# A folded weight made by seven half-block products a row pair, on one Trainium2 core

## The chip, the cores and the metric

The kernel runs on one core of a Trainium2 chip (trn2). A time is the device time of one execution in microseconds, and a comparison is made between medians of runs. A profile shows one execution, taken by the hardware profiler. Its engines are TensorE (PE; PEld is its weight load), VectorE (DVE), ScalarE (ACT), GpSimd (POOL) and SyncE (SP, which issues most of the DMAs).

## The reference, cut to what matters

An mLSTM cell (batch 4, 8 heads, 768 positions, 40 wide) is followed by a feed-forward block with a multiplicative gate. Only the second part is touched by the change:

```python
def _moe_ref(x, w1, w2, w3, w_out):      # x is 3072 x 320, the cell's output
    a = x @ w1                           # 320 x 1024
    b = x @ w2                           # 320 x 1024
    h = a * b @ w3                       # 1024 x 1024
    return (h @ w_out).astype(np.float32)  # 1024 x 320
```

As nothing stands between `@ w3` and `@ w_out`, the kernel multiplies the two weights first. `w3 @ w_out`, 1024 x 320, is the folded weight; each token block is then multiplied by it once. All products are in float32.

## The kernel before, in words

**Steps.** The program is written out by one Python loop over `s`, 32 steps. The cell's work is cut in 24 units (6 stretches of 128 positions for each of 4 batches); step `s` makes the attention-like products of unit `s` and the outputs of unit `s − 1`. These small products of 64x64 quarters of TensorE's array, `quarter_work`, write the tiles `cell`. They stand at the end of a step on TensorE and need, from GpSimd, the weighted values `vw` (line 330), the masked weights `pw` (L308) and decayed states (L335, `decayed`). On VectorE they lead to `h`, `den`, the output `y`, and the states (L404, L414). `x_trans` turns a finished `y` on TensorE into `px`, and ScalarE copies that to `xT`, the feed-forward input.

**Up blocks.** In steps 2 to 15 each step also makes one or two up blocks (`up`, `up_rest`). A block is two of the eight 128-wide parts of the hidden dimension for 256 tokens. `pa` and `pb` collect `x @ w1` and `x @ w2`. The model width is 320 = 128 + 128 + 64: the first two parts are products of 128 rows (`up`), the last 64 rows are four products on 64x64 quarters of the array that run together (`up_rest`, tile `wr`). ScalarE then copies `pa` to `a_sb` (L638), and VectorE multiplies `pb` by it into `ab` (L639). In steps 19 to 30 the up blocks are made in another way, by seven half-block products (`up_by_seven`), and the last output blocks too (`out_by_seven`). Neither is touched.

**Fold.** Weights come by DMA as raw words; ScalarE scales them and VectorE puts them together to float32 (`convert`, L199 and L200), a few in each step by the list `n_cvt`. For `w3` VectorE also turns the block (L248) into `w3T`, of which two are kept, one for each of two 128-row parts `ko`. Some steps later, at the start of a step, `fold` makes 8 products of 128 x 128 by 128 x 320 for each `ko` whose `w3T` is ready, in one PSUM bank `wp`, and ScalarE copies the sum to `w3o` (L264). There are 8 such `ko`; two are folded at the start of step 10 and one in each of the steps 11 to 16. `wo` holds `w_out`, and after the fold its memory serves as workspace.

**Down blocks.** From step 16 on, `ffn_out` multiplies `ab` by `w3o`: 8 products of 320 columns a block of 128 tokens, in a bank `po`, copied by ScalarE to `o_sb` and sent out by its queue.

**Order.** TensorE's instructions are issued in the order of the program text (`in_order`, through the helpers `mm`, L92, and `transpose`, L95). On the other engines a scheduler keeps nearly the order of the text as well; `tc.issue_after` holds a group of instructions behind a named one. Four PSUM banks belong to `cell`, and four are handed out by `mps`, each new tile taking a bank that has been emptied; a tile's first product waits for the engine that emptied that bank. A float32 product of the text is two matmuls and two weight loads in TensorE's stream.

The lines that hand out the work around the change:

```python
n_up = [0] * 2 + [1] * 4 + [2] * 10 + [0] * 16
n_down = [0] * 16 + [2] * 5 + [1] * 4 + [0] * 7
todo = w12[5:] + [("wo", i, 0) for i in range(FO)] + [("w3", ko, part) for ko in range(FO) for part in range(2)]
n_cvt = [0, 0, 2, 0, 1, 2, 3, 3, 3] + [2] * 6
```

Of the kernel before, what the change touches and what calls it, by code (L numbers as in the profile page):

```python
# [8 lines left out]
FP = mybir.dt.float32  # L9
# [3 lines left out]
UP = 2.0 ** 9  # L13
# [3 lines left out]
def kernel(  # L17
# [212 lines left out]
    w3T_t = {}  # L230
    turned_w3, ready_w3 = [], []

# [4 lines left out]
    def convert():  # L237
        if not scaled:
            scale_next()
        dst, raw, ko, half = scaled.pop(0)  # L240
        if dst is not None:
            to_f32(dst, raw)
            return
        w3 = wst.tile([128, CW], FP, name="w3", tag="w3")
        to_f32(w3, raw)
        if half == 0:
            w3T_t[ko] = wst.tile([128, FO, 128], FP, name="w3T", tag="w3T")
        nc.vector.transpose(out=w3T_t[ko].rearrange("c k (m r) -> c m k r", r=32)[:, 2 * half:2 * half + 2],  # L248
                            in_=w3.rearrange("r (m c k) -> r m k c", m=2, k=FO))
        if half:  # L250
            turned_w3.append(ko)

    def fold():
        while ready_w3:
            w3_mm(ready_w3.pop(0))
        ready_w3.extend(turned_w3)
        turned_w3.clear()

    def w3_mm(ko):
        w3T = w3T_t.pop(ko)  # L260
        wp = mps([128, DM], "wp")
        for ki in range(FO):
            mm(wp, w3T[:, ki, :], wo[:, ki, :], start=(ki == 0), stop=(ki == FO - 1))
        nc.scalar.mul(out=w3o[:, ko, :], in_=wp, mul=UP ** -2)  # L264

# [351 lines left out]

    def up(gr, fs, cs):

# [3 lines left out]
        x, n = x_t[gr], cs.stop - cs.start  # L623
        pa, pb = mps([128, len(fs), n], "pa"), mps([128, len(fs), n], "pb")
        for p, wt in ((pa, w1), (pb, w2)):
# [4 lines left out]

    def up_rest(pa, pb, x, gr, fs, cs):
        for i, f in enumerate(fs):
            for j, e in quarters:
                mm((pa, pb)[j][halves[e], i, :], wr[halves[j], f * 128 + e * L:f * 128 + (e + 1) * L],
                   x[halves[j], KF, cs], start=False, stop=(i == len(fs) - 1))
        j, t0 = divmod(cs.start, 2 * P)
# [95 lines left out]

    def ffn_out(blocks, pos=None):

        pos = pos or [mps([P, DM], "po") for _ in blocks]
        for (gr, j), po in zip(blocks, pos):
            for f in range(FO):
                mm(po, ab_t[gr][j // 2][:, f, j % 2 * P:(j % 2 + 1) * P], w3o[:, f, :], start=(f == 0), stop=(f == FO - 1))
        for (gr, j), po in zip(blocks, pos):
            o_sb = ffn.tile([P, DM], FP, name="o_sb", tag="o_sb", bufs=2)  # L740
            nc.scalar.copy(out=o_sb, in_=po)  # L741
            t0 = j * S + gr * P
            nc.scalar.dma_start(out=out[t0:t0 + P, :], in_=o_sb)


    KH, NH = FO // 2, DM // 2

# [9 lines left out]
    T_o, S_o = [], {}  # L757
    wsums = out_weight_sums()

# [53 lines left out]
    todo = w12[5:] + [("wo", i, 0) for i in range(FO)] + [("w3", ko, part) for ko in range(FO) for part in range(2)]  # L813
    n_cvt = [0, 0, 2, 0, 1, 2, 3, 3, 3] + [2] * 6
    n_fetch = [5, 5, 10]
# [4 lines left out]
    for s in range(len(n_up)):  # L820
# [21 lines left out]
        if s < NU:  # L842
            if s >= B:
                decayed(state[s % B][1], state[s % B][0], s, 0)
        if s == 2 or N_DVE < s < NY + 2:
            twice(s - 2)
        if NY <= s - 2 < NU:
            get_back(s - 2)
        while s >= N_DVE and turned < min(s - 2, NY):
            x_trans(turned)  # L850
            turned += 1
        fold()
        if s >= len(n_up) - 2:
# [16 lines left out]
        if seven and s <= NU:  # L870
            ffn_out([downs.pop(0) for _ in range(n_down[s])], [cell[1][:, i, 0:DM] for i in range(2)])
        else:
            for _ in range(n_down[s]):
                ffn_out([downs.pop(0)])
# [4 lines left out]
        now = [ups.pop(0) for _ in range(n_up[s])]  # L879
        open_ups = [up(*x) for x in now] if s != 2 else []  # L880
        if s == 3:
            turn(3)
        def rest():
            for x in open_ups:
                up_rest(*x)
            if seven:
# [5 lines left out]
        def between():  # L892
# [17 lines left out]
            convert()  # L910
            up_rest(*block)

# [3 lines left out]
        else:  # L916
            rest()
        with tc.issue_after(gated.ins) if gated else nullcontext():
            if seven:
                seven[3]()  # L920
            for _ in range({NU: 1, NU + 1: 3}.get(s, 0)):
                next(wsums)
# [41 lines left out]
        if s == B:  # L964
            for i, r in enumerate(third):
                nc.sync.dma_start(out=U_d[i * GC:(i + 1) * GC].rearrange("c r t -> r c t"), in_=U3[r])
        with tc.issue_after(gated.ins) if N_DVE <= s + 1 < NU else nullcontext():
            for _ in range(n_cvt[s] if s < len(n_cvt) else 0):
# [13 lines left out]
    behind.close()  # L982
    assert not ups and not sevens and not downs and not outs and not summed and not todo and not pend and not turned_w3 and not ready_w3, (len(ups), len(downs), len(todo), len(pend))
# [28 lines left out]
```

## Time and profile before

| | us |
|---|---|
| median of 3 runs (lowest, highest) | 426.75 (425.93, 427.64) |
| the profiled execution, its own time | 427.89 |
| span of that execution, first to last instruction | 425.8 |

Busy time of the engines in four stretches of that span:

| stretch, us | PE | DVE | ACT | POOL | DMA share |
|---|---|---|---|---|---|
| 0 to 108 (steps 0 to 9) | 100.98 | 83.34 | 70.04 | 34.64 | 0.91 |
| 108 to 218 (steps 10 to 16) | 109.12 | 80.72 | 41.45 | 24.14 | 0.73 |
| 218 to 334 (steps 17 to 26) | 115.58 | 82.34 | 29.48 | 59.07 | 0.51 |
| 334 to 426 (the rest) | 88.37 | 67.07 | 9.12 | 36.45 | 0.08 |

A busy time is the time in which at least one instruction of the engine was under way. Matmuls overlap, so the mean duration of one says less than the spacing of their starts. "Idle before, releaser" in a row is the time for which the engine stood still ahead of that group, and what ended it; "issue" is a stand for which the profile shows no reason. The fold runs from 108 to 209 us.

### The profile page before, as it was taken

The numbers are of one execution on the slowest core, as the hardware profiler recorded it, in microseconds if no ns is written. First come the engines' busy times: TensorE is split into PE (matmuls) and PEld (weight loads), VectorE is DVE, ScalarE is ACT, GpSimd is POOL, SyncE is SP. The second block draws the span as 40 slices with busy tenths as digits, with TensorE's granted clock in tenths as the row PEclk, the third lists the DMA queues.
The fourth block names the chain that finished last, engine by engine and source line by source line (L and its number), as shares of the span: only waits on it lengthen the run. The fifth ranks groups of instructions, "written<-read, shape, count | busy, mean of one in ns | idle before, by whom it ended". The sixth has DMA issues, their size and how long they took to land.

```text
span 425.8 us, 13079 instructions
## 1 busy us (share of the span) xinstructions
PE 414.1 (97%) x5353; PEld 335.3 (79%) x5353; DVE 313.5 (74%) x635; ACT 150.1 (35%) x404; POOL 154.3 (36%) x211
## 2 busy tenths in 40 slices
PE   7989989999999999999999999999999999999996
PEld 4768878888688788787777778788778879888896
DVE  6676986888949779778736966596868699575971
ACT  4766865567723623630433313032311110210000
POOL 4421342233303303303307751546453587542100
PEclk9989999999999999999999999999999999999999
DMA  8999998598977776985425675756421120000001
GB/s 186 204 173 245 214 144 140 134 193 180 215 183 154 166 182 135 181 164 105 89 80 130 153 141 121 142 133 117 87 44 36 35 39 2 31 2 31 2 32 62
DMA packets 135211, 51.15 MB, mean 120 GB/s; under 512 B 109360, under 2 KB 126960, under 8 KB 135152
## 3 DMA queue, kind: packets, MB, share of 16 engines
q1 hardware_dynamic: 131552, 46.29, 53.9%
q10 hardware_dynamic: 3600, 4.03, 2.7%
q8 instruction: 42, 0.69, 0.7%
q14 instruction: 17, 0.14, 0.1%
HBM read 44.50 MB, written 5.80 MB: 118 GB/s over the span
## 4 chain that ended last, share of the span: by engine, by line
PE 53%; issue 20%; DVE 7%; POOL 7%; SPq 7%; DMA 5%; ACT 1%; POOLq 0%; DVEq 0%
PE cell L92 17%; PE pa L92 12%; PE o L92 8%; PE pb L92 8%; PE p L92 3%; POOL pw L308 3%; SPq L184 3%; DVE w3T L666 2%; PE pt L95 1%; POOL vw L330 1%; SPq L148 1%; DMA raw<-in_moe_w_dram 1%; PE fill L92 1%; POOL raw L659 1%; POOL state L335 1%
## 5 line engine op out<-in xcount | busy, mean ns | idle before, releaser
L335 POOL TENSOR_TENSOR state<-state,decay 128x164 f32<-128x164 f32 x40 | 20.0, 500 | 154.8 <-DVE state L404 129.0
L92 PE MATMUL pa<-xT,w 128*128 128x256 f32 x240 | 60.4, 382 | 0.0
L92 PEld LDWEIGHTS pa<-xT,w 128*128 128x128 f32 x240 | 44.4, 190 | 6.8 <-DVE h L430 0.4
L303 ACT ACTIVATE pw<-pw,aT 128x64 f32<-128x64 f32 x184 | 46.4, 339 | 3.2 <-ACT o_sb L741 1.9
L92 PE MATMUL pb<-xT,w 128*128 128x256 f32 x192 | 45.4, 379 | 0.0
L729 POOL TENSOR_TENSOR ab<-ab,a_sb 128x512 f32<-128x512 f32 x22 | 29.4, 1356 | 32.2 <-DVE ab L684 32.2
L92 PEld LDWEIGHTS pb<-xT,w 128*128 128x128 f32 x192 | 36.4, 190 | 5.0
L711 POOL TENSOR_TENSOR wo<-wo 128x512 f32<-128x512 f32 x22 | 27.4, 1268 | 29.8 <-DVE wo L686 29.8
L92 PE MATMUL pa<-xT,wr 64*64 64x256 f32 x384 | 37.0, 386 | 0.5 <-DVE wr L200 0.5
L92 PE MATMUL wp<-wo,w3T 128*128 128x320 f32 x128 | 35.9, 433 | 1.1 <-DVE ab L639 0.6
L308 POOL TENSOR_SCALAR_AFFINE_SELECT pw<-pw 64x512 f32<-64x512 f32 x48 | 35.8, 746 | 3.0 <-ACT pw L303 1.2
L92 PE MATMUL pb<-xT,wr 64*64 64x256 f32 x384 | 36.4, 380 | 0.0
L92 PE MATMUL cell<-w3o,ab 128*128 128x320 f32 x128 | 35.4, 432 | 0.0
L638 ACT ACTIVATE a_sb<-pa 128x512 f32<-128x512 f32 x24 | 14.3, 598 | 59.0 <-PE pb L92 59.0
L639 DVE TENSOR_TENSOR ab<-pb,a_sb 128x512 f32<-128x512 f32 x24 | 16.4, 688 | 23.2 <-ACT a_sb L638 22.8
L92 PEld LDWEIGHTS wp<-wo,w3T 128*128 128x128 f32 x128 | 23.8, 190 | 10.5 <-DVE ab L639 0.8
L92 PEld LDWEIGHTS cell<-w3o,ab 128*128 128x128 f32 x128 | 24.3, 190 | 9.5
L92 PEld LDWEIGHTS pa<-xT,wr 64*64 64x64 f32 x384 | 18.9, 132 | 15.4 <-issue 8.8
L686 DVE SCALAR_TENSOR_TENSOR a_sb<-pa,wo 128x512 f32<-128x512 f32 x12 | 8.3, 689 | 29.8 <-PE pa L92 29.8
L430 DVE TENSOR_TENSOR h<-cell,h 64x164 f32<-64x164 f32 x88 | 28.6, 326 | 1.6
L92 PE MATMUL po<-w3o,ab 128*128 128x320 f32 x96 | 26.4, 433 | 0.0
L92 PEld LDWEIGHTS po<-w3o,ab 128*128 128x128 f32 x96 | 18.1, 190 | 7.3
(180 smaller groups left out, 846.4 us busy)
## 6 DMA issues: line engine op xcount, KB each, us to landing
raw<-in_moe_w_dram SPq DMA_DIRECT2D x64, 128.0 KB, 3.4
kbuf<-in_k_dram SPq DMA_DIRECT2D x24, 160.0 KB, 4.5
v_all<-in_v_dram SPq DMA_DIRECT2D x24, 160.0 KB, 4.9
o_in<-in_o_gate_dram SPq DMA_DIRECT2D x24, 160.0 KB, 4.8
pw<-U_d SPq DMA_DIRECT2D x28, 128.0 KB, 3.5
raw<-in_moe_w_dram SPq DMA_DIRECT2D x5, 512.0 KB, 6.7
raw<-in_moe_w_out_dram SPq DMA_DIRECT2D x8, 320.0 KB, 4.1
gates<-in_k_dram SPq DMA_DIRECT2D x28, 80.0 KB, 2.5
```

Of the source, the lines that this page charges most:

```text
L92: in_order(nc.tensor.matmul(out, lhsT=lhsT, rhs=rhs, start=start, stop=stop))
L184: nc.sync.dma_start(out=dst, in_=src)
L303: nc.scalar.activation(out=pw[:, h, :], in_=src[:, h, :], func=AF.Exp, bias=aT[:, c, b * H + h:b * H + h + 1])
L308: nc.gpsimd.affine_select(out=pw[r], in_=pw[r], compare_op=OP.is_ge, fill=0.0, base=0, pattern=[[0, H], [1, L]], channel_multiplier=-1)
L335: nc.gpsimd.tensor_tensor(out=new, in0=old, op=OP.mult, in1=decay[:, b * NP:(b + 1) * NP, 2 * c + x:2 * c + x + 1] .to_broadcast([P, NP, D1]))
L430: nc.vector.tensor_tensor(out=part, in0=ph[x][halves[e]], in1=part, op=OP.add)
L638: nc.scalar.mul(out=a_sb, in_=pa, mul=UP ** -2)
L639: nc.vector.tensor_tensor(out=ab_t[gr][j][:, fs[0]:fs[-1] + 1, t0:t0 + a_sb.shape[-1]], in0=pb, in1=a_sb, op=OP.mult)
L666: nc.vector.tensor_tensor(out=dst, in0=p, in1=q, op=OP.subtract)
L686: nc.vector.scalar_tensor_tensor(out=out, in0=p, scalar=UP ** -2, in1=q, op0=OP.mult, op1=OP.add)
L711: aside_by.tensor_tensor(out=kept[j][:, 1:4:2], in0=kept[j][:, 1:3], in1=kept[j][:, 3:4].to_broadcast([128, 2, TH]), op=OP.add)
L729: aside_by.tensor_tensor(out=t[:, f:FO:FH, :], in0=t[:, f:FO:FH, :], in1=a, op=OP.mult)
```

## The change

The product of two consecutive 128-row parts of `w3` (a row pair) and `w_out` is cut in 2 x 2 by 2 x 2 half blocks (`A11` to `A22`, `B11` to `B22`). Before, it took eight half-block products for a pair, as sixteen products of 320 columns; now it takes seven, each of four products of 160 columns.

- Sums of weights on both sides are needed. Those of `w_out` (`T1` to `T4`, four of 640 columns) are made by GpSimd after steps 8 and 9; the last of them is made again in another place in step 15. Those of a row pair (`S1` to `S4`, four of 512 columns) are made by GpSimd after steps 9, 11, 13 and 15. `S3` and `T3` overwrite parts of `w3T` and `wo`; the rest lie in `fold_m`, `w3o`, and memory of `ab` and `raw` that is free then.
- `fold_first` makes two products after the quarter work of steps 9, 11, 13, 14; ScalarE copies them to `w3o`.
- `fold_second` makes the other five in steps 10, 12, 14, after the first up block has been finished, and in step 16 between the down blocks. ScalarE copies the products to memory, and five additions, by GpSimd (VectorE in step 16), make the rows of `w3o`. In step 16 the last two of eight parts of the two down blocks wait for them and stand after the quarter work.
- In steps 9, 11 and 13 the banks of the up blocks are handed out as `pa`, `pa`, `pb`, `pb` instead of `pa`, `pb`, `pa`, `pb`.
- In steps 2 to 5 the quarter products of up blocks are split in two of 128 columns each: both parts in steps 2 to 4, the second part alone in step 5.
- One weight conversion moves from step 8 to step 5, the buffer `w3` becomes single, and `o_sb` moves to the memory of `fold_m`.

```diff
-    def fold():
-        while ready_w3:
-            w3_mm(ready_w3.pop(0))
...
-        for ki in range(FO):
-            mm(wp, w3T[:, ki, :], wo[:, ki, :], start=(ki == 0), stop=(ki == FO - 1))
-        nc.scalar.mul(out=w3o[:, ko, :], in_=wp, mul=UP ** -2)
+    def fold_weight_sums():
...
+        for dst, p, q in ((T1, B12, B11), (T2, B22, T1), (T4, B21, T2), (B12, B22, B12)):
+            yield nc.gpsimd.tensor_tensor(out=dst, in0=p, in1=q, op=OP.subtract)
+    def fold_sums(i):
...
+        for dst, p, q, op in ((S1, A21, A22, OP.add), (S2, S1, A11, OP.subtract), (A21, A11, A21, OP.subtract),
+                              (S4, A12, S2, OP.subtract)):
+            nc.gpsimd.tensor_tensor(out=dst, in0=p, in1=q, op=op)
+    def fold_first(i):
...
+        wp = fold_products(((A11, B11), (A12, B21)))
+        return lambda: nc.scalar.mul(out=fold_of(i)[:, 0:3:2], in_=wp, mul=UP ** -2)
+    def fold_last_sum():
...
+        nc.gpsimd.tensor_tensor(out=B21, in0=B21, in1=fold_T[1], op=OP.subtract)
+    def fold_second(i):
...
+        wp, wq = mps([128, 3, NH], "wp"), mps([128, 2, NH], "wq")
+        for p, x, a, b, first, last in ((wq, 1, A22, T4, True, False), (wp, 0, S1, T1, True, False), (wp, 1, S2, T2, False, False),
+                                        (wp, 2, S3, T3, False, True), (wq, 0, S4, B22, False, True)):
+            for k in range(KH):
+                mm(p[:, x], a[:, k, :], b[:, k, :], start=(first and k == 0), stop=(last and k == KH - 1))
...
+        nc.scalar.mul(out=M1, in_=wp, mul=UP ** -2)
+        nc.scalar.mul(out=M2, in_=wq, mul=UP ** -2)
+        def adds(by=nc.gpsimd):
+            for out, p, q in ((C[:, 1], M1[:, 1], C[:, 0]), (C[:, 0], C[:, 0], C[:, 2]), (C[:, 2], M1[:, 2], C[:, 1]),
+                              (C[:, 1:4:2], C[:, 1:3], M1[:, 0:1].to_broadcast([128, 2, NH])), (C[:, 1:3], M2, C[:, 1:3])):
+                by.tensor_tensor(out=out, in0=p, in1=q, op=OP.add)
...
+    def up_banks(n):
+        shape = [128, 2, 2 * P]
+        return zip(*[[mps(shape, name) for _ in range(n)] for name in ("pa", "pb")])
...
+            parts = split[i]
+            n = (cs.stop - cs.start) // parts
+            for t in range(parts):
+                for j, e in quarters:
+                    mm((pa, pb)[j][halves[e], i, t * n:(t + 1) * n], wr[halves[j], f * 128 + e * L:f * 128 + (e + 1) * L],
...
-    n_cvt = [0, 0, 2, 0, 1, 2, 3, 3, 3] + [2] * 6
+    n_cvt = [0, 0, 2, 0, 1, 3, 3, 3, 2] + [2] * 6
...
+        elif s == 16:
+            finish = ffn_out([downs.pop(0) for _ in range(n_down[s])], split=FO - 2)
+            fold_second(FO // 2 - 1)(nc.vector)
...
+        if s in (10, 12, 14):
+            up_rest(*up(*now.pop(0)))
+            adds.append(fold_second((s - 10) // 2))
+        if s != 2:
+            open_ups = [up(*x, pair) for x, pair in zip(now, up_banks(len(now)) if s in (9, 11, 13) else [None] * len(now))]
...
+        if s in (9, 11, 13):
+            x_trans(turned)
+            turned += 1
+        if s in (9, 11, 13, 14):
+            first_copy = fold_first((s - 8) // 2)
...
+            if s in (8, 9):
+                next(fsums), next(fsums)
+            for x in adds:
+                x()
+            if s in (9, 11, 13, 15):
+                fold_sums((s - 9) // 2)
```

## The prediction

> **What bounds the kernel now.** Read first the page's busy times and queues, then TensorE in order of time.
>
> ```profile
> PE 414.1 (97%) x5353; PEld 335.3 (79%) x5353; DVE 313.5 (74%) x635; ACT 150.1 (35%) x404; POOL 154.3 (36%) x211
> ...
> q8 instruction: 42, 0.69, 0.7%
> ```
>
> TensorE is busy for 97% of the span and the others far less, so a microsecond taken from its stream counts wherever the next wait is not already due. TensorE's timeline in the stretch where the weight is folded (start us, us, engine, line, operation, tiles, shapes, count, idle time before and its releaser):
>
> ```profile
> 107.22 0.55 PE L95 MATMUL px<-ident,y 128*128 128x128 f32 x3
> 108.35 8.88 PE L92 MATMUL wp<-wo,w3T 128*128 128x320 f32 x32 [0.58 <-DVE ab L639]
> 117.06 1.89 PE L92 MATMUL pa<-xT,w 128*128 128x256 f32 x8
> ...
> 128.04 4.47 PE L92 MATMUL wp<-wo,w3T 128*128 128x320 f32 x16
> 132.35 1.89 PE L92 MATMUL pa<-xT,w 128*128 128x256 f32 x8
> ...
> 144.57 3.93 PE L92 MATMUL wp<-wo,w3T 128*128 128x320 f32 x14 [0.54 <-issue]
> ```
>
> One product of the source is two matmuls. Sixteen of 320 columns last from 128.04 to 132.35, 4.31 us or 0.269 us each; work follows without a gap. Two gaps stand here: 0.58 us for VectorE, 0.54 us of "issue". The price of 160 columns is in the last stretch:
>
> ```profile
> 401.78 2.34 PE L92 MATMUL o<-gates,pw 128*128 128x160 f32 x16
> 403.96 1.25 PE L92 MATMUL o<-w3o,ab 128*128 128x160 f32 x8
> ```
>
> Sixteen take 403.96 − 401.78 = 2.18 us, 0.136 us each: half the columns, half the time. Going in and out of the 64x64 quarter products has a price too:
>
> ```profile
> 364.67 0.59 PE L92 MATMUL pa<-w3T,w 128*128 128x256 f32 x2
> 365.10 0.59 PE L92 MATMUL pb<-xT,raw 128*128 128x256 f32 x2
> 365.63 1.09 PE L92 MATMUL pa<-xT,wr 64*64 64x256 f32 x16
> ...
> 367.51 0.70 PE L92 MATMUL p<-xT,w 128*128 128x256 f32 x2
> 368.05 0.59 PE L92 MATMUL p<-w3T,raw 128*128 128x256 f32 x2
> ```
>
> Pairs follow every 0.43 us. Into the quarters it is 0.53 (+0.10); the 32 quarters (eight groups of four, 0.215 us each in their own rows) take 1.88 instead of 1.72 (+0.16); the pair after takes 0.54 (+0.11). One excursion costs 0.37 us. And the early steps show a stop in the middle of equal instructions:
>
> ```profile
> 57.17 0.40 PE L92 MATMUL cell<-vw,kbuf 64*40 64x41 f32 x20
> 59.05 0.35 PE L92 MATMUL cell<-vw,kbuf 64*40 64x41 f32 x12 [1.49 <-issue]
> ```
>
> No data is awaited there. 5353 matmuls and as many loads in 42 packets of queue q8 are some 255 instructions a packet: TensorE ran out of instructions.
>
> The last views are GpSimd's groups and the end of a step on VectorE and GpSimd:
>
> ```profile
> L755 POOL TENSOR_TENSOR gates<-w3o 128x640 f32<-128x640 f32 x1 | 2.0, 1986 | 0.0
> L755 POOL TENSOR_TENSOR v_all<-w3o 128x640 f32<-128x640 f32 x1 | 1.5, 1545 | 0.0
> L711 POOL TENSOR_TENSOR wo<-wo 128x512 f32<-128x512 f32 x22 | 27.4, 1268 | 29.8 <-DVE wo L686 29.8
> ```
> ```profile
> 130.37 0.47 POOL L335 TENSOR_TENSOR state<-state,decay 128x164 f32<-128x164 f32 x1 [13.93 <-DVE state L404]
> ```
>
> **What the Trainium skill says.** *Runtime: NRT & Kernel Launch*, "Instruction fetch mechanics": instructions come in blocks of 16 KiB, 256 at a time, fetched ahead, at a cost that is "mostly hidden". The 42 packets agree; the 1.49 us is a case that wasn't hidden. *TensorEngine Tiling (Array Packing)*, "Key Properties": changing the tiling mode drains TensorE; the 0.37 us agrees. *GPSIMD Engine Reference*, "Elementwise": a two-input operation is about twice as slow as on VectorE; L711 agrees (1268 ns against 693 on VectorE). *SBUF — State Buffer*, "two separate sides": GpSimd and a two-input VectorE operation exclude each other on a shared port; L755, 1545 or 1986 ns for one shape, fits.
>
> **The change, part by part.** E is the end of a step's quarter work on TensorE.
>
> *Products.* Out: 8 rows x 16 matmuls x 0.269 = 34.5 us. In: 4 row pairs x 7 products x 4 x 2 = 224 matmuls x 0.136 = 30.4. On the path: **−4.1 us**.
>
> *Order.* In steps 10, 12 and 14 the second products stand between two up blocks, so the quarter products of the first block are an excursion of their own: 3 x 0.37 = **+1.1**. Bounds +0.8 to +1.3.
>
> *Banks.* `px` and `wp` after steps 9, 11, 13 get banks that ScalarE or the earlier VectorE product empties, and step 8 has a `w3` conversion less (0.43 + 0.69 + 1.11 us) queued on VectorE ahead of the ab product that `wp` waited for. The 0.58 goes, **−0.5** (0 to −0.6). What is late next there is the copy of `px`, which nothing after it on TensorE needs for 7 us.
>
> *GpSimd's sums.* After step 9 it gets two 640-column differences and four 512-column sums, after 11, 13 and 15 four. They start when L335 above ends: 130.84, 3.2 us after E (127.66, where px starts). By 1545 and 1268 ns: T4 at E+4.8, T3 6.3, S1 7.6, S2 8.8, S3 10.1, S4 11.4. TensorE needs T4 after px 0.4, two products 2.2, pa and pb 3.5 and the excursion 1.1: E+7.1; then S1 at 8.2, S2 9.3, S3 10.4, S4 11.5 (four products' eight matmuls are 1.09). Uncontended they are just in time; with 1986 and 1.6 us they end at 13.6 and the last product is 2.2 late. I take **+0.5** (0 to +2.2). After 11, 13 and 15 there is no T; S4 is at E+8.3, or 9.6: covered. Queued behind the sums are `vw` and the masks (0.7 + 0.2 + 1.8 us), due in step 10 only at E+17: covered. The five adds after 10, 12, 14 (three of 160 columns near the 500 ns of the 164-column row, two of 320 near the 764 of vw) are 3.0 us and put `vw` at E+6.9, the masks at 8.9; needed at 10.5 and 10.3 (px 0.4, up 6.9, quarters 1.9, then half of the cell matmuls). Cover 1.4 us; gone, it would cost what the adds grow beyond that.
>
> *VectorE.* The turning of w3 row 2 now waits for S4, as both use one buffer. Behind it stand a second conversion and the ab product of step 10's first block: free by E+11.4 + 1.1 + 2.3 + 0.7 = 15.5. Its reader is the bank for the px at step 10's end, E+19: 0, cover 3 us. Conversions moved forward to steps 5 and 7 add 1.2 us in each; the idle time before ab products was 2.9 us in step 5 and none in step 7, whose lateness ends before `pa` of the next step needs the bank: 0 (to +0.5). Their weight DMAs move one conversion forward on SP's queue, behind that step's loads and ahead of the next step's, whose data are due two steps later: 0.
>
> *ScalarE.* Eight copies of 0.44 become four of 320, four of 480 and four of 320 columns: about 2.3 us more on an engine 35% busy; pb of the second block waits for the 480-column copy, which has 2.8 us: 0.
>
> *Step 16.* The last sums are made by VectorE (three near 320 ns, two near 490, as L794 and L795): they end 1.7 us after the last product, and the quarter work covers 1.75. The two output DMAs on ScalarE's queue leave some 7 us later, far from the end. 0 (to +0.7).
>
> *Split quarters.* Twice the matmuls of half the columns; even 41 columns stream 32 matmuls in 0.44 us, four in 0.055, below the 0.107 that four of 128 columns need. 0 (to +0.2) in itself; but it adds 112 instructions by step 5, and the fold 192.
>
> *Instructions.* TensorE's visible stops of this kind are 1.49, 0.54, 0.41 and 0.30: 2.7 us. The ends of the packets shift by 112, later by more. Counting along the changed order with the durations above, the last 256 instructions before an end take under 3.5 us at six places (2.15, 2.25, 2.8, 3.2, 3.4, 3.5). At the stop shown, supply took about 4.1 us (the previous end passed at 54.9). Other dense places of before went without a stop. I take **+0.3** (−2 to +6).
>
> Sum: −4.1 + 1.1 − 0.5 + 0.5 + 0.3 = **−2.7 us**. The profiled execution took 427.89 us (span 425.8), 1.14 over the median of 426.75; it would become 425.2, and a median run 424.0.
>
> **Rivals.** (A) The sum as it stands, 424.0; 0.45. (B) GpSimd and VectorE exclude each other as in the 1986 ns row, and TensorE waits 2.2 us in step 10: 425.7; for it speaks the row, against it that VectorE itself idles behind S4 then; 0.25. (C) Slower: instruction supply. At 4.1 us the six places cost 7.3 (2.7 now): −2.7 − 0.3 + 4.6 = +1.6. From 4.2 us on it is past +2.1 (428.9), at 4.5 some **431**. For it: 1.49 us at 57; against: the DMA queues are fuller there than later, and most dense places of before passed; 0.12. (D) The shift puts the ends where TensorE is slow and 2.1 of the 2.7 us go: 421.6; 0.15. (E) The change doesn't give what it says, since weight loads of 190 ns bound the short products: 224 x 0.19 = 42.6, +8, 433; the 0.136 of the tail speaks against it; 0.03.
>
> **How the numbers follow.** A measurement of this kernel can tell about 0.5%, 2.1 us, from no change. A lies under 424.6 in seven parts of ten (0.32), with D and a little of B 0.50 faster; the rest of A and most of B 0.35 the same; C and E 0.15 slower. The range, 421.4 to 427.8, reaches from D to beyond B with its bounds, and leaves out most of C and E.
>
> **What would show it.** 160-column wp and wq matmuls near 0.136 us apart; three quarter excursions more; S4 landing near its product in step 10 alone; no wait of wp for VectorE. It is wrong if wq or wp wait for GpSimd in steps 12 or 14, if cell matmuls wait for vw or masks, or if "issue" stops add up to over 5 us.

## The result, and the profile after

The changed kernel takes **428.60 us** in the median of 16 runs (426.32 to 430.46), the kernel before 426.19 (16 runs beside it). The ratio is **1.005, 95% interval 1.0029 to 1.0071**: slower by about 2.4 us, where 424.0 had been forecast. The profiled execution took 429.36 us, its span is 427.6.

The page after, busy times and TensorE's instruction queue:

```profile
PE 411.9 (96%) x5505; PEld 341.6 (80%) x5505; DVE 327.7 (77%) x640; ACT 152.1 (36%) x408; POOL 200.2 (47%) x247
...
q8 instruction: 43, 0.70, 0.8%
```

TensorE is busy for 2.2 us less than before and the span is 1.8 us longer: the work went down, the waits went up. VectorE's busy time rose by 14.2 us although it got only five instructions more (the additions of step 16, some 2 us together). That is the first hint.

To place the difference, compare the starts of each step's first `cell<-qT,kT` matmul in the two traces. From step 9 to step 17, where the fold lies, the changed kernel needs **3.12 us more**; from 17 on the two run alike to 0.02 us. Up to step 9 it is 1.30 us ahead, but there the profiles of kernels that are alike up to step 8 differ by nearly 4 us, so that part says little. The stretches between these starts that end in steps 10, 12 and 14 got longer (+2.7, +4.1, +5.1 us), those that end in steps 11 and 13 shorter (−4.0, −4.3), as the change says; the sum should have been negative.

TensorE's timeline at the first fold (columns as in the prediction):

```profile
105.92 0.55 PE L95 MATMUL px<-ident,y 128*128 128x128 f32 x3
108.31 2.44 PE L92 MATMUL wp<-wo,w3T 128*128 128x160 f32 x16 [1.85 <-DVE ab L712]
110.59 1.89 PE L92 MATMUL pa<-xT,w 128*128 128x256 f32 x8
...
115.16 1.35 PE L92 MATMUL wq<-w3o,w3T 128*128 128x160 f32 x8
117.16 2.71 PE L92 MATMUL wp<-fold_m,ab 128*128 128x160 f32 x16 [0.64 <-POOL ab L284]
119.93 1.35 PE L92 MATMUL wp<-wo,w3T 128*128 128x160 f32 x8
121.63 1.35 PE L92 MATMUL wq<-wo,ab 128*128 128x160 f32 x8 [0.35 <-POOL ab L284]
122.82 1.89 PE L92 MATMUL pa<-xT,w 128*128 128x256 f32 x8
```

The 0.58 us for VectorE was to go; it became 1.85, and in the table of waits it is there three times (us in total, times, longest):

```profile
PE wp L92 <- DVE ab L712: 3.8, 3, 1.8
...
PE wp L92 <- POOL ab L284: 0.6, 1, 0.6
```

The other two stand before steps 12 and 14; the first of them:

```profile
140.41 0.55 PE L95 MATMUL px<-ident,y 128*128 128x128 f32 x3
141.79 2.44 PE L92 MATMUL wp<-wo,w3T 128*128 128x160 f32 x16 [0.84 <-DVE ab L712]
```

Why VectorE is late for the first one is seen by laying its rows beside those of GpSimd. VectorE before, in the same step, where GpSimd makes no sums:

```profile
98.35 0.76 DVE L443 SCALAR_TENSOR_TENSOR o_in<-o_in,den 128x320 f32<-128x320 f32 x1
99.15 0.49 DVE L445 TENSOR_TENSOR y<-h,o_in 128x320 f32<-128x320 f32 x1
...
107.65 1.24 DVE L639 TENSOR_TENSOR ab<-pb,a_sb 128x512 f32<-128x512 f32 x2
```

VectorE after:

```profile
98.58 1.58 DVE L508 SCALAR_TENSOR_TENSOR o_in<-o_in,den 128x320 f32<-128x320 f32 x1
100.19 1.73 DVE L510 TENSOR_TENSOR y<-h,o_in 128x320 f32<-128x320 f32 x1
101.84 0.95 DVE L199 TENSOR_SCALAR w<-raw 128x512 uint32<-128x512 uint32 x1
102.93 1.10 DVE L200 CUSTOM_DVE_ANT_0 w<-raw,w 128x1024 uint16<-128x1024 uint16 x1
...
107.61 1.25 DVE L712 TENSOR_TENSOR ab<-pb,a_sb 128x512 f32<-128x512 f32 x2
```

GpSimd after:

```profile
98.26 1.55 POOL L266 TENSOR_TENSOR fold_m<-wo 128x640 f32<-128x640 f32 x1
99.89 1.68 POOL L266 TENSOR_TENSOR fold_m<-wo,fold_m 128x640 f32<-128x640 f32 x1
101.53 0.98 POOL L395 TENSOR_TENSOR vw<-v_all,wT 128x328 f32<-128x328 f32 x1
...
115.55 1.56 POOL L284 TENSOR_TENSOR ab<-w3T 128x512 f32<-128x512 f32 x1
117.18 1.27 POOL L284 TENSOR_TENSOR ab<-ab,w3T 128x512 f32<-128x512 f32 x1
118.43 1.45 POOL L284 TENSOR_TENSOR w3T<-w3T 128x512 f32<-128x512 f32 x1
119.83 1.74 POOL L284 TENSOR_TENSOR ab<-w3T,ab 128x512 f32<-128x512 f32 x1
```

`o_in` ends at 100.16, `y` at 101.92: within 0.35 us of the ends of GpSimd's two differences (99.81, 101.57). Each of the two takes as long as the GpSimd operation beside it. By this `o_in` and `y` lose 0.82 and 1.24 us, and the first conversion is longer than the next one (0.95 and 1.10 beside `vw` and the masks, against 0.43 and 0.69). The ab products (L712) start at 107.61 as the last of this queue, and `wp` gets its bank from the first of them. Before, they started 0.43 us after `px` (107.65 and 107.22), behind three conversions; now 1.69 us after it (107.61 and 105.92), behind two. The second products then go at GpSimd's pace: their groups start at 117.16, 119.93, 121.63, each right behind the end of the sum it reads (117.11, 119.88, 121.57).

### The profile page after: what moved, and what is told of

The parts are those of the page before. It is cut to its first block, busy times and chain, and to the rows that moved or that the text cites. A ratio compares the mean times of both kernels' runs of the same rounds, so it can differ in the third digit from the quotient of the medians.

```text
span 427.6 us, 13443 instructions
## 1 busy us (share of the span) xinstructions
PE 411.9 (96%) x5505; PEld 341.6 (80%) x5505; DVE 327.7 (77%) x640; ACT 152.1 (36%) x408; POOL 200.2 (47%) x247
## 4 chain that ended last, share of the span: by engine, by line
PE 69%; DVE 11%; SPq 9%; DMA 4%; issue 3%; ACT 1%; POOL 1%; DVEq 0%; POOLq 0%
PE cell L92 19%; PE pa L92 16%; PE pb L92 10%; PE o L92 8%; PE wp L92 5%; PE p L92 4%; PE po L92 4%; SPq L139 3%; SPq L184 3%; PE wq L92 2%; DVE w3T L739 2%; DVE w L200 2%; SPq L153 1%; DMA wo<-in_moe_w_dram 1%; DVE pw L856 1%
## 5 line engine op out<-in xcount | busy, mean ns | idle before, releaser
L92 PE MATMUL pa<-xT,wr 64*64 64x256 f32 (+1 forms) x412 | 37.7, 372 | 0.5 <-DVE wr L200 0.5
L92 PE MATMUL pb<-xT,wr 64*64 64x256 f32 (+1 forms) x412 | 37.1, 366 | 0.0
L92 PEld LDWEIGHTS pa<-xT,wr 64*64 64x64 f32 x412 | 19.9, 132 | 15.6 <-issue 9.8
L712 DVE TENSOR_TENSOR ab<-pb,a_sb 128x512 f32<-128x512 f32 x24 | 15.8, 673 | 10.1 <-ACT a_sb L711 10.0
L92 PEld LDWEIGHTS pb<-xT,wr 64*64 64x64 f32 x412 | 21.1, 133 | 3.0
L395 POOL TENSOR_TENSOR vw<-v_all,wT 128x328 f32<-128x328 f32 x24 | 19.5, 814 | 5.3 <-DMA v_all<-in_v_dram 4.0
```

The source lines that it names most:

```text
L92: in_order(nc.tensor.matmul(out, lhsT=lhsT, rhs=rhs, start=start, stop=stop))
L395: nc.gpsimd.tensor_tensor(out=vw_t[n], in0=vbuf[n % NBV], op=OP.mult, in1=wT[:, c, b * H:(b + 1) * H].unsqueeze(2).to_broadcast([P, H, D1]))
L712: nc.vector.tensor_tensor(out=ab_t[gr][j][:, fs[0]:fs[-1] + 1, t0:t0 + a_sb.shape[-1]], in0=pb, in1=a_sb, op=OP.mult)
```

## The experiments

Two theories stand against each other. **P**: the sums on GpSimd hold the port that it shares with VectorE, VectorE is late, and `wp` waits. **S**: the fold moved from every step into the even ones; an odd step is now too short for what VectorE has to do in it, sums or no sums. A third, **I**, is instruction supply: what changes is where the instruction packets end. For each run I give the ratio to before, and from its profile the difference to before from step 9 to step 17 ("the region"; +3.12 in the changed kernel). A kernel whose TensorE stream is shifted can differ there by 2 to 3 us though nothing in the region was edited, as the last two runs show. The runs that test P and S keep the stream of the kernel that they are compared with.

**No sums** (`fold_weight_sums`, `fold_sums`, `fold_last_sum`).

This kernel leaves the sums out: its products read the blocks as they are, and its output is not that of the reference.

```diff
-        fold_T.extend((T1, T2, B12, T4))
-        for dst, p, q in ((T1, B12, B11), (T2, B22, T1), (T4, B21, T2), (B12, B22, B12)):
-            yield nc.gpsimd.tensor_tensor(out=dst, in0=p, in1=q, op=OP.subtract)
+        fold_T.extend((B11, B22, B12, B21))
...
-        fold_S[i] = S1, S2, A21, S4
+        fold_S[i] = A21, A22, A21, A22
...
-            nc.gpsimd.tensor_tensor(out=dst, in0=p, in1=q, op=op)
...
-        nc.gpsimd.tensor_tensor(out=B21, in0=B21, in1=fold_T[1], op=OP.subtract)
```

> The changed kernel without GpSimd's 21 sums of weights (T and S; the second products read the unsummed blocks, so this part of the computation is left out); products, copies and the adds stay. Theory P (the sums shut VectorE's two-input operations out of the shared port; VectorE comes late, and wp waits for its ab product): the three waits of wp (1.8, 0.8, 1.1 us in the changed kernel) and the two waits of the second products for GpSimd (0.6, 0.3) go for the most part, about 424 us, 0.995 of the kernel before. Rival Q (VectorE is late through its own queue: the moved conversions, the single w3 buffer): the waits of wp stay, 427.5 or more. Rival M (modes and short products cost TensorE more than worked out): the waits go and the time stays above 427.

Measured: 423.99 us, ratio **0.9931 (0.9906 to 0.9956)**; region −1.53. In step 8 `o_in` and `y` are back at 0.76 and 0.49 us, and the wait before step 10 is gone. VectorE's busy time is 315.9 us instead of 327.7, so most of the 14.2 us was made by the sums. But two waits of 1.2 us are left, before steps 12 and 14; in the steps ahead of them, 11 and 13, the changed kernel makes no sum either. So the sums are part of the cost, some 4.6 us (their own pace, in step 10, included), and not the whole. VectorE in step 11 of this run:

```profile
121.92 0.69 DVE L708 TENSOR_TENSOR ab<-pb,a_sb 128x512 f32<-128x512 f32 x1 [5.24 <-ACT a_sb L707]
...
126.92 0.70 DVE L506 TENSOR_TENSOR y<-h,o_in 128x320 f32<-128x320 f32 x1
...
131.34 1.13 DVE L247 STREAM_TRANSPOSE w3T<-w 128x512 f32<-128x512 f32 x1
...
134.87 1.25 DVE L708 TENSOR_TENSOR ab<-pb,a_sb 128x512 f32<-128x512 f32 x2
```

And TensorE at the end of that step:

```profile
133.87 0.55 PE L95 MATMUL px<-ident,y 128*128 128x128 f32 x3
135.57 1.63 PE L92 MATMUL wp<-wo,w3T 128*128 128x160 f32 x10 [1.16 <-DVE ab L708]
```

VectorE works from 121.92 with hardly a break until the first of the two ab products ends at about 135.5: 13.6 us, of which 5.4 are two `w3` conversions with their turns. TensorE's odd step lasts 11.0 us now; before, it lasted 15.3. This is where S was formed. The same work, to the end of the second turn, takes 13.0 us here and took 12.3 before: the conversions lie beside `vw` and the masks, which GpSimd's additions have pushed back (0.75 and 1.11 us for the first, 0.43 and 0.69 before), and the single `w3` delays the second. Both have a share: at the 12.3 us of before some 0.5 us of each wait would be left (an estimate), and at a step of 15.3 us there was none. A run without the additions was not made.

**Before, with GpSimd loaded.** The old fold, plus differences of the same sizes in the same places on GpSimd, into a tile that nobody reads; `w3` single as in the changed kernel.

```diff
+    def idle_sums(n, c):
+        for i in range(n):
+            nc.gpsimd.tensor_tensor(out=load_m[:, 0:c], in0=w1[:, 0, 0:c], in1=w1[:, 1, 0:c], op=OP.subtract)
...
-        w3 = wst.tile([128, CW], FP, name="w3", tag="w3")
+        w3 = wst.tile([128, CW], FP, name="w3", tag="w3", bufs=1)
...
+            if s in (8, 9):
+                idle_sums(2, 2 * DM)
+            if s in (10, 12, 14):
+                idle_sums(3, DM // 2)
+                idle_sums(2, DM)
+            if s in (9, 11, 13, 15):
+                idle_sums(4, 512)
```

> The kernel before with GpSimd operations of the same number and sizes in the same places (640-column pairs after steps 8 and 9, four of 512 columns after 9, 11, 13, 15, three of 160 and two of 320 after 10, 12, 14), on data that nobody uses, and with the single w3 buffer. P: VectorE's y chain grows after those steps, the first wp waits 2 us or more instead of 0.58, 427.5 to 429. Q and M: as the kernel before, 426.2 within 0.7.

Measured: 429.08 us, ratio **1.0059 (1.0036 to 1.0083)**; region +2.93. TensorE at the first fold:

```profile
105.30 0.55 PE L95 MATMUL px<-ident,y 128*128 128x128 f32 x3
108.04 3.32 PE L92 MATMUL wp<-wo,w3T 128*128 128x320 f32 x6 [2.19 <-DVE ab L644]
```

The old products wait in the same place, 2.19 us where before had 0.58, with `o_in` at 1.57 and `y` at 1.73 us. No result of these GpSimd operations is read by anyone. VectorE's busy time is 327.6 us, that of the changed kernel, with not one instruction more than before. The single `w3` has a share: a conversion starts 1.21 us after the start of the turn before it, not 1.06, twice 0.15 us of the 1.6 us by which VectorE is later. Work on GpSimd that nothing waits for makes this kernel slower through VectorE: P is shown. All of it falls in step 10 (+3.31; the region has 0.4 less, as a part of the "issue" gap of before in step 12 is missing here). Steps 11 to 16 have their loads too, and none of them is longer than before: at 15.3 us each they have the room.

**The sums later in the step.** All T sums, the S sums and the additions are issued behind `vw` and the masks.

```diff
-            if s in (8, 9):
-                next(fsums), next(fsums)
...
             if s != 2:
                 out_gate(s)
+        if s == 8:
+            for _ in range(4):
+                next(fsums)
+        for x in adds:
+            x()
+        if s in (9, 11, 13, 15):
+            fold_sums((s - 9) // 2)
```

> The changed kernel with GpSimd's sums and adds queued behind vw and the masks of the step instead of ahead (all four sums of w_out after step 8), so that they start about 3 us later, when VectorE has finished y. P: L508 and L510 are back near 0.76 and 0.5 us, the waits of wp shrink from 3.8 us in sum to under 2, 425 to 427. Q: they stay and so does the time, 428.6. It may lose up to 1 us where the second products now wait for later sums.

Measured: 430.62 us, ratio **1.011 (1.0066 to 1.0155)**; region +4.35. A miss. `o_in` and `y` are fast again (0.77 and 0.49 us), but the sums now fall on the conversions (1.19 and 1.82 us, where alone they take 0.43 and 0.69), `wp` waits for VectorE as long as in the changed kernel (3.7 us in sum, 3.8 there) and longer for GpSimd (1.7 in sum, 0.6 there). Moving the sums within a step only chooses which of VectorE's operations stands still.

**Conversions dealt out anew** (S alone).

```diff
-    n_cvt = [0, 0, 2, 0, 1, 3, 3, 3, 2] + [2] * 6
+    n_cvt = [0, 0, 2, 0, 1, 3, 3, 3, 2] + [3, 1] * 3
```

The entry for step 9 is a 3; its conversions are issued at the end of that step and made while TensorE is in the long step 10.

> The changed kernel with the conversions of the folds of steps 10 to 15 dealt out anew: each short odd step makes one of them, each long even step three (two each before). Theory S (the steps are uneven: with the fold's products in the even steps an odd step lasts some 11 us on TensorE, and VectorE needs some 13 us from its E to the ab product whose bank wp takes): wp's waits of about 1.2 us each in steps 12 and 14 go, the one in step 10 stays (1.5 to 2 us), so about 2.3 us less, 426 to 427 us where the changed kernel has 428.6, and from step 9 to 17 about 0.8 us more than before instead of 3.1. Theory P (the port that VectorE and GpSimd share is the whole cost): the sums lie in step 9 alone, so nothing changes, 428 to 429 us. A rival to both: the second products of the even steps now wait for the conversions that were moved there, and the time is the changed kernel's or over it, with waits of wq for DVE w3T in steps 10, 12 and 14.

Measured: 425.55 us, ratio **0.998 (0.9963 to 0.9998)**; region −0.12. One line of a list brings back 3.2 us of the region. The wait before step 10 stays at 1.83; before steps 12 and 14 `wp` follows `px` at once:

```profile
141.84 0.55 PE L95 MATMUL px<-ident,y 128*128 128x128 f32 x3
142.22 2.34 PE L92 MATMUL wp<-wo,w3T 128*128 128x160 f32 x16
```

No second product waits for a conversion in steps 10, 12 and 14, so the rival of this run falls. S is shown in this sense: one conversion less in an odd step ends its wait, with GpSimd's work left as it was. The gain is larger than I expected, 3 us and not 2.3.

**Neither sums nor unevenness.** The first and the last edit together; the sums are left out here too.

> The kernel without GpSimd's T and S sums (left out; the products read unsummed blocks) and with the conversions dealt out anew. Both causes taken away together: no wait of wp for VectorE over 0.5 us is left in steps 10, 12 and 14, and from step 9 to 17 the prediction's two terms stand alone, -4.1 for the products and +1.1 for the excursions, so -3 to -4 us there and 421.5 to 423 us in all. If the short products or the excursions cost more than I worked out (theory M), the region keeps the -1.5 us of the run without sums, and the time stays at 424 though the waits are gone.

Measured: 421.81 us, ratio **0.9868 (0.9838 to 0.9898)**; region −4.2. With both taken away nothing of `wp` or `wq` waits:

```profile
103.83 0.55 PE L95 MATMUL px<-ident,y 128*128 128x128 f32 x3
104.22 2.34 PE L92 MATMUL wp<-wo,w3T 128*128 128x160 f32 x16
106.39 1.89 PE L92 MATMUL pa<-xT,w 128*128 128x256 f32 x8
...
110.96 1.35 PE L92 MATMUL wq<-wo,w3T 128*128 128x160 f32 x8
112.15 3.42 PE L92 MATMUL wp<-wo,w3T 128*128 128x160 f32 x24
115.41 1.25 PE L92 MATMUL wq<-wo,w3T 128*128 128x160 f32 x8
116.50 1.89 PE L92 MATMUL pa<-xT,w 128*128 128x256 f32 x8
```

Sixteen matmuls of 160 columns take 106.39 − 104.22 = 2.17 us, 0.136 each. The five products take 5.54 us here and 7.66 (115.16 to 122.82) in the changed kernel: the pace of GpSimd costs 2.1 us in step 10. The four kernels make a square, in us of the region:

| | conversions 2, 2 | conversions 3, 1 |
|---|---|---|
| sums on GpSimd | +3.12 | −0.12 |
| no sums | −1.53 | −4.2 |

The sums cost 4.1 to 4.7 us, the unevenness 2.7 to 3.2, and the two nearly add up. All four have the same matmuls in the same order, and no stop for "issue" over 0.2 us in the region.

**Sums on VectorE**, on top of the new list of conversions: T and S by `nc.vector`, the four T sums all after step 9.

```diff
-            yield nc.gpsimd.tensor_tensor(out=dst, in0=p, in1=q, op=OP.subtract)
+            yield nc.vector.tensor_tensor(out=dst, in0=p, in1=q, op=OP.subtract)
...
-            nc.gpsimd.tensor_tensor(out=dst, in0=p, in1=q, op=op)
+            nc.vector.tensor_tensor(out=dst, in0=p, in1=q, op=op)
...
-            if s in (8, 9):
-                next(fsums), next(fsums)
+            if s == 9:
+                for _ in range(4):
+                    next(fsums)
```

> The kernel with the conversions dealt out anew, and GpSimd's T and S sums put on VectorE, all after step 9's conversions; the additions of the last fold stay on GpSimd. Theory P: with GpSimd quiet in step 9, VectorE's own o_in and y are back at 0.76 and 0.5 us and the first wp waits about 1 us or less; the sums themselves cost VectorE about 21 x 0.7 = 15 us inside steps 9 and 10, of which the part that the second products wait for is 0 to 2 us. Sum: 423 to 425 us, under both kernels. Rival (VectorE has no room: it has about 1 to 2 us of slack in each step of this region): the sums push the second products of step 10, and then the ab product of step 12, back by 3 to 6 us, and the time is 428 to 432.

Measured: 424.85 us, ratio **0.9961 (0.9941 to 0.998)**; region −1.0. This version beats both kernels. VectorE makes a T sum in 0.82 us and an S sum in 0.69 to 0.94:

```profile
111.70 0.82 DVE L266 TENSOR_TENSOR fold_m<-wo 128x640 f32<-128x640 f32 x1
...
115.68 0.94 DVE L284 TENSOR_TENSOR ab<-w3T 128x512 f32<-128x512 f32 x1
```

`o_in` and `y` are at 0.76 and 0.49 us. What is left of the sums is 3.2 us of the region against the run without them. In step 10 and at its end TensorE waits 0.91 us ahead of `wq`, 0.78 for a sum and 0.97 for the ab product whose bank `px` takes: VectorE lacks time there.

**The same, with sums and products in alternating order.**

```diff
-        for dst, p, q in ((T1, B12, B11), (T2, B22, T1), (T4, B21, T2), (B12, B22, B12)):
+        for dst, p, q in ((T1, B12, B11), (T2, B22, T1), (B12, B22, B12), (T4, B21, T2)):
...
+            if not i:
+                next(fsums)
             nc.vector.tensor_tensor(out=dst, in0=p, in1=q, op=op)
...
-        for p, x, a, b, first, last in ((wq, 1, A22, T4, True, False), (wp, 0, S1, T1, True, False), (wp, 1, S2, T2, False, False),
-                                        (wp, 2, S3, T3, False, True), (wq, 0, S4, B22, False, True)):
+        for p, x, a, b, first, last in ((wp, 0, S1, T1, True, False), (wp, 1, S2, T2, False, False), (wp, 2, S3, T3, False, True),
+                                        (wq, 1, A22, T4, True, False), (wq, 0, S4, B22, False, True)):
```

> The kernel with the sums on VectorE and the conversions dealt out anew (0.9961 of before), with one more edit: the first T and S sums alternate, and the second products take them in that order, the one with T4 fourth and not first; the banks as they were. There, at the start of step 10's second products, TensorE waited 0.9 us for wq (T4, the third sum) and 0.8 us for wp (S1). If these are waits for single sums, the first product can start after two of them (T1 and S1) and the last still waits for S4, which comes when it came: 0.5 to 0.9 us less, 423.9 to 424.4 us. Rival (the sums as a block are what VectorE lacks time for, so the end of step 10's products is set by S4 whatever the order): 424.5 to 425.2, and the wait stands ahead of the last product in place of the first.

Measured: 424.93 us, ratio **0.9959 (0.9939 to 0.9979)**, the same as without the edit; region −1.33. The two waits at the start turned into 0.53 and 0.25 us further on, and that of `px` for the ab product at the end of step 10 grew from 0.97 to 1.52. The rival held in the time; the wait went to `px`, not to the last product.

**The bank edit made effective.** In the changed kernel `wp` has the bank of the step's first `pb`. Without the edit of `up_banks` the program has the same instructions in the same order on every engine, and every tile in the same bank: in this program a pool's banks follow the order of first use, and not the order in which the text asks for them. So this part of the change is void. Here four pools of one bank each make it real:

```diff
-    ps_m = ctx.enter_context(tc.tile_pool(name="ps_m", bufs=4, space=bass.MemoryType.PSUM))
+    four = [ctx.enter_context(tc.tile_pool(name=f"ps_m{i}", bufs=1, space=bass.MemoryType.PSUM)) for i in range(4)]
...
-    banks = [ps_m]
+    banks = list(four)
```

> The changed kernel with the bank edit made effective: four PSUM pools of one bank each, so that the bank follows the order in which the program hands it out (px gets the first pa's bank and wp the second pa's, both emptied by ScalarE; in the changed kernel wp has the bank of the first pb, which VectorE empties). Theory B (wp waits for VectorE's ab product only because of the bank that it is given): wp's waits in steps 10, 12 and 14, 3.8 us, go or shrink to what the next up block's pa then waits for the same product, which comes 2.2 us later behind wp's 16 instructions; so 2 to 3.5 us less, 425 to 426.5. Rival: VectorE is the bound in these steps whatever bank wp has, and the wait only moves to the next pa: 428 to 429.

Measured: 434.21 us, ratio **1.0181 (1.0125 to 1.0236)**; region +9.0. The `wp` that follows `px` does not wait for VectorE any more (0.1 us after the last `px` matmul), but the fixed rotation gives the second block of steps 10, 12 and 14 the two banks of the first, and its `pb` now waits for the ab product of the same step:

```profile
PE pb L92 <- DVE ab L712: 5.4, 3, 2.3
```

The wait moved and grew. **With the same pools on the version with alternating sums:**

> The kernel with the sums on VectorE and the conversions dealt out anew, with two more edits: the first T and S sums alternate and the second products read them in that order (the product with T4 comes fourth, not first), and the banks follow the order of the program. The kernel without these two stood at 0.996 of before, with waits of 0.9 and 0.8 us at the start of step 10's second products and 1.0 us of px for the ab product after it. If both edits take their waits away: 1.5 to 2.5 us less, 422 to 423.5 us. Rival (VectorE has no slack in steps 9 and 10, each sum that is not waited for here is waited for by the ab product at the end of step 10): 424.5 to 425.5, as without them.

Measured: 440.76 us, ratio **1.0341 (1.0288 to 1.0393)**: there the ab product of step 10 stands behind eight sums, and `pb` waits 12.8 us in three places; region +13.7. As the pools also tie all other tiles to a rotation, these two runs show that VectorE's lateness reaches TensorE through another bank as well; they do not price the edit that was meant.

**Quarters whole again, in the changed kernel.**

```diff
-                up_rest(*x, split=(2 if s in (3, 4, 5) else 1, 2 if s in (3, 4) else 1))
+                up_rest(*x)
...
-            up_rest(*block, split=(2, 2))
+            up_rest(*block)
```

> The changed kernel with the quarter products of steps 2 to 5 whole again. Theory I (the place of the instruction packets decides): a stop of 1 us or more appears or goes, and the time moves by 1 to 2 us. P: the fold region stays as it is (+3 us against before between steps 9 and 17), the total within 1 us of the changed kernel, 428.6.

Measured: 429.85 us, ratio **1.0083 (1.0051 to 1.0115)**; region +2.83. The interval overlaps that of the changed kernel, so by itself it decides nothing. Its profile has an "issue" stop of 1.60 us at 161 us that the changed kernel lacks.

**Quarters split, in the kernel before** (the diff above the other way round, with `up_rest` of the changed kernel).

> The kernel before with only the quarter products of steps 2 to 5 split by columns. By the prediction this costs 0 to 0.2 us. The changed kernel with whole quarters was slower than the changed kernel by about 0.3% (1.0083 against 1.005, intervals overlapping), which would make it a gain of about 1 us here: 425 to 426 where before has 426.1. If it is nothing: 426 to 426.5. Instruction supply (more packets in the same time) as a cost would show as 427 to 429 with longer stops of TensorE's instructions in steps 2 to 6.

Measured: 428.74 us, ratio **1.0046 (1.0024 to 1.0067)**: 2 us slower, where the edit should cost 0 to 0.2 and the run above had made it look like a gain; region +2.30, though nothing in the region was edited. Its profile has a stop in the fold, and none over 0.15 us in the steps of the edit:

```profile
157.08 0.43 PE L92 MATMUL cell<-vw,kbuf 64*40 64x41 f32 x25
158.76 0.28 PE L92 MATMUL cell<-vw,kbuf 64*40 64x41 f32 x7 [1.25 <-issue]
```

**Before, with the same shift of the stream and whole quarters.**

```diff
-                    warm(1, small=38)
+                    warm(3)
```

> The kernel before with 36 warm-up instructions fewer ahead of step 2 (three warm-ups of 512 columns instead of one and 38 of 64x64): 72 matmul rows and 72 weight loads less in TensorE's stream, so that from step 6 on it stands 144 rows earlier, which modulo 256 is the place where the 112 more rows of the kernel with the split quarters put it. Nothing else is changed. Theory I (what a change of the stream's length does is to move the ends of instruction packets over the work): from step 6 on the stops lie where they lie in the kernel with the split quarters (one of 1.2 us in the cell work at about 157 us, none at 57), and the time is 427.5 to 429 where before has 426. Rival (the split quarters themselves cost 2 us): 425 to 426.5, before's own time or, for the shorter warm-up, a little less.

Measured: 428.25 us, ratio **1.0039 (1.0014 to 1.0065)**; region +2.96. The stop is there to the instruction:

```profile
159.51 0.43 PE L92 MATMUL cell<-vw,kbuf 64*40 64x41 f32 x25
161.19 0.28 PE L92 MATMUL cell<-vw,kbuf 64*40 64x41 f32 x7 [1.24 <-issue]
```

After 25 of the same 32 matmuls, for 1.24 us against 1.25, in two kernels of which only one has split quarters, while both have the stream shifted by the same count modulo 256; and the stop of 1.49 us at 57 is gone in both. Theory I holds for the place of the stops, and the split itself is not what costs. Counting matmuls makes it plainer. Over the profiles of all runs but the two with pools of one bank, TensorE's "issue" stops of 0.2 us and more stand behind 218, 345, 598, 851, 977, 1608, 2244, 2371, 2499, 3008 or 3136 matmuls of the kernel's own stream, give or take one. From one place to the next it is 126 to 128 matmuls or a multiple, and a packet holds some 256 instructions (twice 5505 in 43), a matmul and a load by turns. The place is fixed; whether there is a stop, and how long, is not: behind matmul 851 five kernels with the same stream up to there stop for 0.30 to 1.58 us, and two do not. This profile also has a single stop of 3.79 us, from 39 us on, at such a place (597). Part of the 2 us in both runs is of another kind: at the start of step 10 `pa` waits 0.9 and 1.6 us for `xT`, which ScalarE copies behind a conversion that waits for its load. Whether that comes from the shift too was not tried.

## Why the prediction was wrong

Summed over the region, the terms of the prediction (products, order, banks, sums) gave −3.0; it came out as +3.1.

- **VectorE 0: the step that failed.** The prediction costed the work that VectorE gets and gives away, and held the rest as it was. Two things happened to the rest. Its operations beside the sums got longer: the prediction had the fact (the Trainium skill's *SBUF — State Buffer*, "two separate sides") and used it only for GpSimd's durations, but it works the other way too, `o_in` 0.76 to 1.58 us, `y` 0.49 to 1.73. And VectorE was checked against the end of step 10, which is long, not against those of steps 11 and 13, which the change makes 4.3 us shorter. From the last `px` matmul to `wp` it is 2.12, 1.11 and 1.43 us in the changed kernel, where 0.11 is the spacing without a wait: 4.3 us of waiting for the ab product, 2.3 of it in the last two. Before had 0.7. So it is **+3.6 instead of the −0.5 of the banks and the 0 of VectorE**, and "no wait of `wp` for VectorE", which was named as a sign, did not come.
- **Banks −0.5: right for step 10 but for that, and half of its reason void.** Without the sums, and with one conversion less in step 8, the ab product starts 1.35 us earlier against TensorE's step than before, and the wait is gone. With them it starts 1.26 us later. No bank was changed by the edit: `wp` follows the first ab product of the step, before as after. The prediction allowed for that product and took it to be early. The copy of `px`, named as late next, was not late in the changed kernel.
- **Products −4.1 and order +1.1: right.** In the run without sums and unevenness the stretches that end in steps 11 and 13 are 4.30 us shorter than before, one row of 4.31. The one that ends in step 14 is 3.66 longer: 56 matmuls at 0.136 (7.6 us) and one excursion of 0.37 in place of one row are 3.66. So 0.136 us a matmul and 0.37 an excursion both hold, and rival E (weight loads) is out; its 433 was wrongly summed as well, 12.2 us over A are 436. The −4.2 of that run holds, to within 0.2, these −3.0, the 0.7 of `wp`, and the 0.7 by which the "issue" gap at 144 us lengthens a step of before; both waits are gone there.
- **GpSimd's sums +0.5: mis-sized; +2.1**, in step 10 alone, as expected. This is within 0.1 of rival B's 2.2 us, but by luck in part. The six sums take 9.3 us (112.26 to 121.57), midway between the two paces of the prediction (8.2 and 10.4). They start 6.3 us after `px`, not 3.2: GpSimd waits for VectorE's state first. The row that the prediction read is that of the end of step 10; at the end of step 9, behind one conversion more, before has:

```profile
111.87 0.46 POOL L335 TENSOR_TENSOR state<-state,decay 128x164 f32<-128x164 f32 x1 [9.60 <-DVE state L404]
```

It ends 5.1 us after `px` (107.22). TensorE, held up by `wp`, came 2.1 us late itself, and that hid a part. In steps 12 and 14 no second product waits for GpSimd, as worked out.

- **ScalarE 0, step 16 0: right.** TensorE waits for ScalarE nowhere in the region for over 0.15 us. The stretch that ends in step 17 is 2.27 us longer, of which 2.15 are the eight matmuls of 320 columns that were moved behind the quarter work. From step 17 on the kernels run alike; the end is level with step 17 to 0.02 us.
- **Split quarters 0: right in itself; instructions +0.3: within its range, but of a kind I had priced too tamely.** In the changed kernel the stops are 0.41 us at 18, 1.05 at 50 and 0.20 at 193, 1.1 us less than before's 2.7. In two other kernels the same shift by 112 rows goes with 1.7 to 2 us. The Trainium skill's *Runtime: NRT & Kernel Launch*, "Instruction fetch mechanics", calls the cost "mostly hidden"; most ends of packets do pass unseen here, but the 1.24, 1.60 and 3.79 us were not hidden.

These pieces come to some +2.0 (−3.0, +3.6, +2.1, and −0.7 for the gap at 144 us that the change moved away). The other 1.1 of the 3.1 lie in 0.1 to 0.4 us a step and are not explained.

The rival that ends slower was instruction supply, and that was not it: the cause was one that I had in hand and did not follow to the other engine.

## What to carry to other kernels

Moving work to an idle GpSimd isn't free for VectorE: find VectorE's operations that will run beside it and have two inputs in SBUF, and those like the conversions here that a trace shows to suffer too; let each end no earlier than the GpSimd operation that it meets, and follow the sum to the next bank that VectorE empties. When a change moves work between steps, check every other engine against the steps that got shorter, not the ones that got longer; here one list of conversions was worth 3 us. And when an edit changes the length of TensorE's stream, expect something like the 2 us that it cost two kernels here, from the ends of instruction packets: an edit worth less than that needs a twin with the same shift to be judged.

## What had not been expected of the hardware

- A 320-column VectorE operation (`y`) of 0.49 us took 1.73 beside a GpSimd operation of 1.68; a conversion with one input (L199) went from 0.43 to as much as 1.19, and the 16-bit one (L200) from 0.69 to 1.82.
- `o_in` takes 0.49 us alone (before, at 325 us). Where it starts beside a GpSimd operation, it ends 0.34 or 0.35 us after that one's end, whatever its length: 0.55 us beside 0.53, 0.76 beside 0.73 (`vw`, before too), 1.33 beside 1.30, 1.58 beside 1.55. So the 0.76 of the kernel before was a wait already.
- Not all of VectorE's work is touched. With an input in PSUM, the ab product takes 0.64 to 0.69 us beside GpSimd or not; the turns (L247, L382), which read SBUF, keep 1.06 to 1.15 (six of the profiles).
- GpSimd work that nothing reads cost 2.9 us in eight steps, 0.6% of the whole time (1.0059).
- A stop of TensorE at the end of an instruction packet can last 3.79 us in one piece; its place follows the count of instructions, its length does not.
